# Decay attention and a spectral mix on one core: the fold's x sum moved to VectorE, 64-row blocks paired, the last unit half by rows, repeats in fp32

## The chip, the cores and the metric

One core of a Trainium2 chip runs the whole program, in one launch. Its engines are TensorE (PE in the profile; its weight loads are PEld), VectorE (DVE), ScalarE (ACT), GpSimd (POOL) and SyncE (SP), each with its own instruction queue, in order. GpSimd and SyncE issue the DMA transfers, which 16 DMA engines carry out. The metric is the device time of the program in microseconds; lower is better. A trace of one profiled execution goes with it.

## The reference

Attention with a decaying bias over 8 batches, 8 heads, 576 positions and head size 64, then a spectral mix over the 512 channels:

```python
scores = q @ k.T / sqrt(64) + (cum[i] - cum[j])      # cum: running sum of log f; causal
x = softmax(scores) @ v                               # (8, 576, 512) over all heads
X = rfft(x, axis=1)[:, :64]                           # 64 modes, Xr and Xi
Yr = Xr @ w_r[m] - Xi @ w_i[m];  Yi = Xr @ w_i[m] + Xi @ w_r[m]     # one 512x512 pair a mode
y = irfft(Y, n=576)
u = x + y
out = u + max(u @ w_ch, 0)
```

w_r and w_i have 64 x 512 x 512 fp32 numbers each, 134 MB together; q, k and v have 28 MB, the output 9.4 MB.

## The kernel before

**Tiles and blocks.** The 576 positions are four blocks of 128 and one of 64 (`SBLK`, block index sb or sc, 0 to 4). Heads go in pairs; `pairs` lists 32 of them, g over the four head pairs (128 channels each), b over the batches inside. x lies in `x_all[128, g, b, block, 128]` in bf16. Weights come in units of four modes (u, 0 to 15) and quarters of the 512 input channels (dc, 0 to 3). All loads are cast from fp32 to bf16 on the way.

**Order.** The schedule is written by hand: each engine runs its instructions in the order in which the Python text makes them.

**Attention stage** (L597 to L667, 34 iterations). Iteration i first issues loads on GpSimd (`load_qk(i + 4)`, one or two halves of a weight quarter by `issue_half`, `load_v(i + 3)`). Then come, interleaved: `trans` (q and k turned by PE, copied to `qkT` by VectorE, L391), `scores` (PE L466, exponential by ScalarE L473), `turn_v` (v turned into `tv` by PE, L413, and copied to `vT` by VectorE, L415; `vT` has one buffer), `back_v` (PE turns `vT` back block by block, L424 and L431, the 64-row block in two pieces; ScalarE copies to `vs`, L435), `av` (scores times values for the pair before), `norm` (VectorE divides by the row sums into `x_all`, L529), `dft` (PE, L545 and L566: the modes of x) and, from iteration 10, `spec_early`: weight quarters that are already there are multiplied into partial sums kept in `yacc`. The 64-row block of each batch lies in rows 0 to 63.

**Loads.** `wseq` is the order of the weight quarters. `issue_w` issues one quarter as one transfer of 1024 KB (in bf16), or in halves in the attention stage; the very last one in four parts, one a mode. `cuts` splits three quarters at a row. At most eight transfers of GpSimd's are under way: each issue waits for the landing of the one eight before.

**Spectral stage** (L844 to L932). For each unit the remaining quarters are multiplied as they land (`spec_mms`, PE L230: eight matmuls that write rows of A; the last unit uses `spec_cols`, PE L242: 32 matmuls that write columns). VectorE adds the early partial sum (Yb, L901), PE turns the result (L906), VectorE copies it to `YT` or `YLa` (L915, L918). Meanwhile `xw(b)` computes XW = x @ w_ch for each batch. From unit 12 on, ahead of each quarter but the last, `folds` works off a list: for each batch `fold_modes` (y_sb and yw_sb: the first 96 spectral columns and their product with w_ch, PE L754 and L765, ScalarE copies L762 and L773), then for each block `fold_u` (PE adds x by an identity matmul, L781, and the 96 columns, L784; ScalarE copies the sum back to `x_all`, L791) and, one block later, `fold_z` (PE L800; VectorE adds to XW, L807). Their PSUM results use four banks (`psX`). `SHARE`, `PART` and `MODES` say how much of the list each call takes. `place` puts the 64-row blocks of two batches into the lower and upper half of one block, here for the results only.

**The last quarter** comes in four parts. Between the parts PE does the identity matmuls of the first output steps (`base_mm`, L701), each several times over ("repeats": the result of the last counts). When the last part has been multiplied, VectorE adds it to the sums (L889, `accT`), and PE turns the last 32 spectral columns (`last_modes`).

**Output stage** (L1003 to L1045, 18 steps of two blocks). U = x + y and Z = u @ w_ch are completed on PE (`base`: x or XW by an identity matmul; `rest`: the last columns, L966), ScalarE copies U (L1000), VectorE makes max(Z, 0) + U (L1030), SyncE issues the store (L1045). In the steps of `late_x` one block's x is not added by PE but by GpSimd (L1035); in those of `by_pool` GpSimd makes one block's final sum (L1025).

Of the kernel before, what the change touches and what calls it, by code (L numbers as in the profile page):

```python
# [23 lines left out]
def kernel(  # L24
# [11 lines left out]
    nc = tc.nc  # L36
# [46 lines left out]
    wT = const.tile([128, NPAIR, 9], BF16, name="wT")  # L83
# [62 lines left out]
    cuts = {(4, 2): 30, (7, 2): 20, (10, 2): 20}  # L146
# [5 lines left out]
    def issue_w(half=None):  # L152
# [29 lines left out]
        elif half != 1:  # L182
            src = (moe_w_r, moe_w_i)[dc - 2]
            parts = [(0, 4, 0, 128)]
            if n + 1 == len(wseq):
                parts = [(j, 1, 0, 128) for j in range(4)]
            elif (u, dc) in cuts:
                n0 = cuts[(u, dc)]
                parts = [(0, 4, 0, n0), (0, 4, n0, 128)]
# [86 lines left out]
    nc.vector.tensor_scalar(s_f[:], s_f[:], float(S - 1), None, ALU.min)  # L276
# [30 lines left out]
    def setup_w():  # L307
# [7 lines left out]
        for hp in range(2):  # L315
            half = slice(64 * hp, 64 * hp + 64)
            nc.scalar.activation(wT[:, :, hp:8:2], cbg[:, :, 0:4, hp], ACT.Exp, scale=-1.0)
            nc.scalar.activation(wT[half, :, 8], cbg[half, :, 4, hp], ACT.Exp, scale=-1.0)
# [88 lines left out]
    def turn_v(i):  # L407

        tv = psM.tile([128, 9, 64], BF16, tag="m", name="tv")
        for r in range(9):  # L410
# [3 lines left out]
        st[i]["vT"] = vTpool.tile([128, S], BF16, tag="vT", name="vT")  # L414
        nc.vector.tensor_copy(  # L415
            st[i]["vT"][:].rearrange("p (c r) -> p c r", r=9), tv[:].rearrange("p r c -> p c r")
        )

    def back_v(i):

        vT = st[i]["vT"]
        vp = psM.tile([128, 9, Dh], BF16, tag="m", name="vp")
        for jb in range(4):
            nc.tensor.transpose(  # L424
                vp[:, 2 * jb : 2 * jb + 2, :].rearrange("p h d -> p (h d)"),
                vT[:, jb * 128 : jb * 128 + 128],
                ident_bf[:, :],
            )
        for hp in range(2):
            sl = slice(64 * hp, 64 * hp + 64)  # L430
            nc.tensor.transpose(vp[sl, 8, :], vT[sl, 512:576], ident_bf[sl, sl])  # L431
        vs = vspool.tile([128, 9, Dh + 1], BF16, tag="vs", name="vs")
        st[i]["vs"] = vs
        nc.vector.tensor_copy(vs[:, :, Dh : Dh + 1], _strided(wT[:, widx(i), :], [[1, 9], [1, 1]]))
# [8 lines left out]
    def scores(i, T):  # L443

        QT, KT = st[i]["T"][:, 0, :], st[i]["T"][:, 1, :]
        if T == 0:
            st[i]["et"] = epool.tile([128, 3, 2, 512], BF16, tag="et", name="et")
            st[i]["e4"] = epool.tile([128, 64], BF16, tag="e4", name="e4")
# [53 lines left out]

    def av(i, sb):
# [6 lines left out]
        Ms = SBLK[sb]  # L510
        for hp in range(2):
            for jb in range(sb + 1):
                rhs = vs[:, 8, :] if jb == 4 else vs[:, 2 * jb + hp, :]
                nc.tensor.matmul(  # L514
                    pav[:Ms, sb % 3, hp, :],
                    lhsT=eblk(i, hp, jb, sb),
                    rhs=rhs,
# [4 lines left out]
    def norm(i, part):  # L522
        g, b = pairs[i]
        pav = st[i]["pav"]
        for ns, lo, hi in ([(128, 0, 3)] if part == 0 else [(128, 3, 4), (64, 4, 5)]):
            n = hi - lo
            rcp = normsb.tile([128, 3, 2, 1], F32, tag="rcp", name="rcp")
            nc.vector.reciprocal(rcp[:ns, 0:n, :, :], pav[:ns, lo % 3 : lo % 3 + n, :, Dh : Dh + 1])
            nc.vector.tensor_tensor(  # L529
                x_all[:ns, g, b, lo:hi, :].rearrange("p s (h d) -> p s h d", h=2),  # L530
                pav[:ns, lo % 3 : lo % 3 + n, :, 0:Dh],
                _strided(rcp[:ns, 0:n, :, :], [[2, n], [1, 2], [0, Dh]]),
# [3 lines left out]
    def dft(i):  # L536
        g, b = pairs[i]
        if g < 2:
            pd = psM.tile([128, 3, 3, ML], F32, tag="m", name="pd")
            half = slice(64 * g, 64 * g + 64)  # L540
            for r in range(3):
                for sc in range(NSB):
                    ns = SBLK[sc]
                    xs = x_all[:ns, g, b, sc, :]
# [3 lines left out]
                        rhs=bas3[:ns, sc, :, ML:NM] if r else bas3[:ns, sc, :, 0:ML],  # L548
# [14 lines left out]
        for r in range(2):  # L563
            for sc in range(NSB):
                ns = SBLK[sc]
                nc.tensor.matmul(  # L566
                    pd[half, r, :, :],
                    lhsT=x_all[:ns, g, b, sc, r:128:2],
                    rhs=bas3[:ns, sc, :, :],
# [9 lines left out]
    def spec_early(u, dc):  # L579
        if u == NU - 1:  # L580
            AT = psM.tile([128, NEB, 8, B], F32, tag="m", name="AT0")
            spec_cols(AT, dc)
            nc.vector.tensor_copy(accT[:], AT[:].rearrange("p e c b -> p e b c"))
            return
# [491 lines left out]
```

## Time and profile before

| What | us |
|---|---|
| runs: all three | 435.54, 437.68, 676.76 |
| median | 437.68 |
| profiled execution | 435.24 |
| its span, first to last instruction | 433.5 |
| attention stage (copies of `vs`, L435, first and last start) | 21.0 to 226.6 |
| fold stretch (first and last L807) | 347.8 to 395.2 |
| first output transfer issued | 404.5 |
| last compute instruction ends | about 427.3 |

```profile
PE 359.8 (83%) x4444; PEld 198.8 (46%) x4444; DVE 265.4 (61%) x651; ACT 228.7 (53%) x374; POOL 143.1 (33%) x214
DMA 46%; PE 33%; DVE 11%; ACT 5%; issue 3%; POOL 1%; DVEq 0%; ACTq 0%; POOLq 0%
HBM read 163.73 MB, written 9.44 MB: 399 GB/s over the span
```

The first line has the busy time of each engine, its share of the span and its instructions; a busy PE is not a PE at its peak, since matmuls overlap. The second is the chain of work that ended last, followed back from the end: what it waited for, as shares of the span. In the answers by window the columns are: start and end, length, then busy us (and instructions) of PE, PEld, DVE, ACT and POOL, the granted TensorE clock (1.00 is full speed), the mean busy share of the 16 DMA engines, and GB/s. In the groups of instructions they are: line, engine, operation, output and inputs, shape and count, then busy us and mean ns of one, then the engine's idle time just before, and who ended it. In the order of time: start, duration, engine, line, operation, count.

### The profile page before, as it was taken

The numbers are of one execution on the slowest core, as the hardware profiler recorded it, in microseconds if no ns is written. First come the engines' busy times: TensorE is split into PE (matmuls) and PEld (weight loads), VectorE is DVE, ScalarE is ACT, GpSimd is POOL, SyncE is SP. The second block draws the span as 40 slices with busy tenths as digits, with TensorE's granted clock in tenths as the row PEclk, the third lists the DMA queues.
The fourth block names the chain that finished last, engine by engine and source line by source line (L and its number), as shares of the span: only waits on it lengthen the run. The fifth ranks groups of instructions, "written<-read, shape, count | busy, mean of one in ns | idle before, by whom it ended". The sixth has DMA issues, their size and how long they took to land.

```text
span 433.5 us, 10703 instructions
## 1 busy us (share of the span) xinstructions
PE 359.8 (83%) x4444; PEld 198.8 (46%) x4444; DVE 265.4 (61%) x651; ACT 228.7 (53%) x374; POOL 143.1 (33%) x214
## 2 busy tenths in 40 slices
PE   1689999988898899999987396599899599989992
PEld 0456666655665565665653132244343233434330
DVE  5788888776878797787785121222222256654893
ACT  4567667777775567667561022023133166752882
POOL 6444444444544444444304112112111212101272
PEclk9999999999999999999999589589799689999997
DMA  8999999999999999999999999999999999998597
GB/s 182 205 233 220 230 223 231 223 231 232 229 230 231 227 233 228 232 229 231 232 218 212 212 212 211 212 210 212 212 211 212 212 212 212 211 212 151 212 380 283
DMA packets 60785, 96.80 MB, mean 223 GB/s; under 512 B 4160, under 2 KB 29248, under 8 KB 60736
## 3 DMA queue, kind: packets, MB, share of 16 engines
q0 software_dynamic: 55040, 85.64, 103.9%
q1 hardware_dynamic: 5696, 10.47, 6.7%
q8 instruction: 35, 0.57, 0.5%
q14 instruction: 14, 0.11, 0.1%
HBM read 163.73 MB, written 9.44 MB: 399 GB/s over the span
## 4 chain that ended last, share of the span: by engine, by line
DMA 46%; PE 33%; DVE 11%; ACT 5%; issue 3%; POOL 1%; DVEq 0%; ACTq 0%; POOLq 0%
DMA w<-in_moe_w_i_dram 31%; DMA w<-in_moe_w_r_dram 13%; PE pd L545 5%; PE sps L466 5%; PE pav L514 5%; DVE qkT L391 4%; PE pd L566 3%; PE A L230 3%; ACT et L473 3%; PE tv L413 3%; DVE vT L415 2%; DMA qk<-in_k_dram 2%; DVE x_all L529 2%; PE Z L701 2%; PE U L701 2%
## 5 line engine op out<-in xcount | busy, mean ns | idle before, releaser
L473 ACT ACTIVATE et<-sps 128x1024 bf16<-128x1024 f32 x96 | 93.1, 1024 | 11.9 <-PE sps L466 10.1
L514 PE MATMUL pav<-vs,et 128*128 128x65 bf16 (+1 forms) x896 | 50.2, 195 | 15.6 <-ACT e L460 15.1
L514 PEld LDWEIGHTS <-et 128*128 128x128 bf16 (+1 forms) x896 | 38.8, 101 | 34.6 <-issue 32.6
L391 DVE COPY qkT<-tp 128x640 bf16<-128x640 bf16 x64 | 48.9, 765 | 4.0 <-PE tp L386 4.0
L901 DVE TENSOR_TENSOR Yb<-A,yx 128x512 bf16<-128x512 f32 x15 | 10.4, 692 | 60.0 <-PE A L230 59.9
L415 DVE COPY vT<-tv 128x576 bf16<-128x576 bf16 x32 | 24.2, 757 | 34.6 <-PE tv L413 33.9
L741 PE MATMUL pxw<-wch,xT 128*128 128x512 bf16 (+1 forms) x160 | 41.7, 417 | 0.0
L466 PE MATMUL sps<-qkT 64*128 64x512 bf16 (+4 forms) x320 | 38.8, 306 | 1.3 <-DVE qkT L391 1.1
L435 ACT COPY vs<-vp 128x576 bf16<-128x576 bf16 x32 | 20.4, 638 | 36.2 <-PE vp L431 36.2
L192 POOL DMA_DIRECT2D w<-in_moe_w_r_dram x19 | 13.9, 731 | 76.5 <-PE A L230 62.6
L529 DVE TENSOR_TENSOR x_all<-pav,rcp 128x384 bf16<-128x384 f32 (+2 forms) x96 | 36.2, 377 | 3.4
L230 PE MATMUL A<-w,XP 128*16 128x512 bf16 (+1 forms) x240 | 22.3, 453 | 19.0 <-DMA w<-in_moe_w_i_dram 11.8
L386 PE MATMUL tp<-ident_bf,qk 128*64 128x128 bf16 x576 | 29.3, 231 | 10.4 <-DMA qk<-in_k_dram 10.1
L748 ACT CAST XW<-pxw 128x512 bf16<-128x512 f32 (+1 forms) x16 | 9.3, 584 | 46.5 <-PE pxw L741 46.5
L748 ACT CAST yx<-pxw 128x512 bf16<-128x512 f32 (+1 forms) x24 | 14.0, 584 | 33.1 <-PE pxw L741 33.1
L112 POOL DMA_DIRECT2D qk<-in_q_dram x32 | 19.5, 608 | 34.1 <-PE tp L386 8.1
L791 ACT CAST x_all<-pu 128x512 bf16<-128x512 f32 (+1 forms) x40 | 23.4, 584 | 13.6 <-PE pu L784 12.9
L192 POOL DMA_DIRECT2D w<-in_moe_w_i_dram x19 | 13.4, 704 | 43.0 <-PE A L230 36.6
L741 PEld LDWEIGHTS <-xT 128*128 128x128 bf16 (+1 forms) x160 | 15.7, 108 | 22.6 <-issue 9.0
L112 POOL DMA_DIRECT2D qk<-in_k_dram x32 | 19.4, 605 | 18.1 <-DMA w<-in_moe_w_i_dram 5.9
L386 PEld LDWEIGHTS <-qk 128*64 128x64 bf16 x576 | 19.0, 113 | 13.6 <-issue 9.6
L403 DVE TENSOR_TENSOR vn<-vt,wn 128x576 bf16<-128x576 f32 x32 | 23.8, 744 | 1.9 <-ACT wn L328 1.9
(158 smaller groups left out, 693.9 us busy)
## 6 DMA issues: line engine op xcount, KB each, us to landing
w<-in_moe_w_i_dram POOLq DMA_DIRECT2D x19, 1024.0 KB, 31.6
w<-in_moe_w_r_dram POOLq DMA_DIRECT2D x13, 1024.0 KB, 29.5
w<-in_moe_w_r_dram POOLq DMA_DIRECT2D x23, 512.0 KB, 11.2
w<-in_moe_w_i_dram POOLq DMA_DIRECT2D x19, 512.0 KB, 11.0
out_dram<-o_sb SPq DMA_DIRECT2D x36, 256.0 KB, 2.8
vt<-in_v_dram POOLq DMA_DIRECT2D x29, 288.0 KB, 10.7
qk<-in_q_dram POOLq DMA_DIRECT2D x32, 144.0 KB, 10.7
qk<-in_k_dram POOLq DMA_DIRECT2D x32, 144.0 KB, 10.6
```

The source lines that it names most:

```text
L112: nc.gpsimd.dma_start(qk[64 * n : 64 * n + 64, :, :], src[b, 2 * g : 2 * g + 2, :, :].rearrange("h (p r) d -> p h (r d)", p=64),)
L192: nc.gpsimd.dma_start(w8[p0:p1, j : j + step, :, :].rearrange("p m r e -> p m (r e)"), src[m : m + step, 256 + 2 * p0 : 256 + 2 * p1, :].r ...
L230: nc.tensor.matmul(A[32 * j : 32 * j + M, :], lhsT=lhsT, rhs=rhs, start=st_, stop=sp_)
L386: nc.tensor.transpose(tp[64 * hp : 64 * hp + 64, r - r0, :, :].rearrange("p n c -> p (n c)"), qk[:, hp, r * 64 : r * 64 + 64], ident_bf[:, :],
L391: nc.vector.tensor_copy(st[i]["T"][:].rearrange("p n (c r) -> p n c r", r=9)[:, :, :, r0:r1], tp[:, 0 : r1 - r0, :, :].rearrange("p r n c ...
L403: nc.vector.tensor_tensor(vn[:], st[i]["vt"][:], _strided(wn[:, widx(i), :], [[1, 9], [0, Dh]]), ALU.mult)
L415: nc.vector.tensor_copy(st[i]["vT"][:].rearrange("p (c r) -> p c r", r=9), tv[:].rearrange("p r c -> p c r"))
L466: nc.tensor.matmul(ps[:, hp, c : c + n], lhsT=KT[sl, jb * 128 : jb * 128 + 128], rhs=QT[sl, i0 : i0 + n], start=True, stop=True,)
L473: nc.scalar.activation(st[i]["et"][:, T, :, :], ps[:], ACT.Exp, scale=scale)
L514: nc.tensor.matmul(pav[:Ms, sb % 3, hp, :], lhsT=eblk(i, hp, jb, sb), rhs=rhs, start=(jb == 0), stop=(jb == sb),)
L529: nc.vector.tensor_tensor(x_all[:ns, g, b, lo:hi, :].rearrange("p s (h d) -> p s h d", h=2), pav[:ns, lo % 3 : lo % 3 + n, :, 0:Dh], _stri ...
L741: nc.tensor.matmul(pxw[rows, :], lhsT=xT[:, eb, sb * 128 : sb * 128 + Ms], rhs=wch[:, eb, :], start=(eb == 0), stop=(eb == NEB - 1),)
```

## The change

Seven edits:

- `fold_u`: the identity matmul and ScalarE's copy go; VectorE adds the PSUM result to `x_all` in place. The 64-row blocks of two batches are folded as one block of 128 rows (`modes_to` makes two matmuls for it), in `fold_u` and in `fold_z`.
- For this `place` holds from the attention on: odd batches have their 64-row block in rows 64 to 127 of the even batch's block. `vT` gets 64 more columns, a copy of its last 64 made by GpSimd, so that `back_v` is five full transposes; `wT` and `vs` have ten parts instead of nine; the basis is set up for both halves. `xw` takes a 64-row pair with the odd batch (640 columns or 512 in place of 576).
- The last unit: quarters 0 and 1 by rows (`spec_mms`) into an fp32 sum Yf, turned by four fp32 matmuls (`ypf`) into `accT`; quarters 2 and 3 by columns as before.
- Repeats: `again`, an fp32 matmul of 256 columns, in place of repeated bf16 ones.
- `late_x` has three more steps: 4, 7 and 16.
- `cuts`: two quarters in three parts in place of three quarters in two.
- `SHARE` 19.1 in place of 19.8, with the pairs put into the list behind their odd batch.

```diff
-    cuts = {(4, 2): 30, (7, 2): 20, (10, 2): 20}
+    cuts = {(5, 3): (54, 126), (8, 3): (63, 78)}
...
-        st[i]["vT"] = vTpool.tile([128, S], BF16, tag="vT", name="vT")
+        st[i]["vT"] = vTpool.tile([128, S + 64], BF16, tag="vT", name="vT")
...
+        nc.gpsimd.tensor_copy(st[i]["vT"][:, S : S + 64], st[i]["vT"][:, S - 64 : S])
...
-        for jb in range(4):
+        for jb in range(NSB):
             nc.tensor.transpose(
...
-        for hp in range(2):
-            sl = slice(64 * hp, 64 * hp + 64)
-            nc.tensor.transpose(vp[sl, 8, :], vT[sl, 512:576], ident_bf[sl, sl])
...
-        Ms = SBLK[sb]
+        rows, _ = place(pairs[i][1], sb)
...
-                    pav[:Ms, sb % 3, hp, :],
+                    pav[rows, sb % 3, hp, :],
...
+            def modes_to(ps, b, sb, which):
+
+                for c in (b, b + 1) if sb == NSB - 1 else (b,):
+                    rows, _ = place(c, sb)
+                    nc.tensor.matmul(
+                        ps[rows, :],
+                        lhsT=BI[:KF, sb * 128 : sb * 128 + SBLK[sb]],
+                        rhs=ys[c][which][:KF, :],
+                        start=True,
+                        stop=True,
+                    )
+
             def fold_u(b, sb):
 
-                Ms = SBLK[sb]
-                rows, to = place(b, sb)
                 pu = psX.tile([128, D], F32, tag="x", name="pu")
-                nc.tensor.matmul(
-                    pu[rows, :], lhsT=ident_bf[:Ms, :Ms], rhs=x_all[:Ms, :, b, sb, :], start=True, stop=False
-                )
...
-                nc.scalar.copy(
-                    x_all[rows, :, to, sb, :], pu[rows, :].rearrange("p (g c) -> p g c", g=NEB)
-                )
+                modes_to(pu, b, sb, 0)
+                xb = x_all[:, :, b, sb, :]
+                nc.vector.tensor_tensor(xb, pu[:].rearrange("p (g c) -> p g c", g=NEB), xb, ALU.add)
 
             def fold_z(b, sb):
...
+                modes_to(pz, b, sb, 1)
+                nc.vector.tensor_tensor(XW[b][:, sb, :], pz[:], XW[b][:, sb, :], ALU.add)
...
-            SHARE = 19.8
-            work = [(b, sb) for b in range(B) for sb in range(-1, NSB)]
+            SHARE = 19.1
+            work = [(b, sb) for b in range(B) for sb in range(-1, NSB - 1)]
+            for p in range(B // 2):
+                work.insert(11 * p + 10, (2 * p, NSB - 1))
...
+            def again(ps):
+
+                nc.tensor.matmul(
+                    ps[:, 0:256], lhsT=ident_f[:], rhs=Yf[:, 0:256], start=True, stop=True
+                )
...
+                        ypf = bank(psT, "ypf")[:, 0 : 64 * NEB].rearrange("p (e c) -> p e c", e=NEB)
+                        for eb in range(NEB):
+                            nc.tensor.matmul(
+                                ypf[:, eb, :],
+                                lhsT=Yf[:, eb * 128 : (eb + 1) * 128],
+                                rhs=perm_f[:],
...
+                        nc.vector.tensor_copy(accT[:], ypf.rearrange("p e (b c) -> p e b c", b=B))
                         U0 = [bank(psT, "U0") for _ in range(2)]
-                        for n in range(4):
-                            base_mm(U0[n % 2], 0, n % 2, 0, True)
-                    if last:
+                    if last and dc == 1:
+                        A = psA.tile([128, D], F32, tag="a", name="A1")
+                        spec_mms(A, u, dc, True, True)
+                        Yf = xtp.tile([128, D], F32, tag="yf", name="Yf")
+                        nc.vector.tensor_tensor(Yf[:], A[:], yacc[u // 2][:, u % 2, :], ALU.add)
+                    elif last:
...
                                 if j == 1:
-                                    for stop in (True, False):
-                                        for k in range(2):
-                                            base_mm(U0[k], 0, k, 0, stop)
+                                    again(U0[0])
+                                    for k in range(2):
+                                        base_mm(U0[k], 0, k, 0)
...
-        late_x = (3, 5, 6, 9, 10, 11, 12, 13, 14)
+        late_x = (3, 4, 5, 6, 7, 9, 10, 11, 12, 13, 14, 16)
```

## The prediction

> **What bounds the kernel now.** I read the page's slices first, then two-microsecond windows around the end, the order of time there, the groups of instructions between 342.5 and 400 us, and the list of DMA issues. The profiled execution took 435.24 us (span 433.5, and 1.7 around it); the three runs shown have a median of 437.68, with 435.54 the lowest. Sums are made on 435.24.
>
> ```profile
> DMA  8999999999999999999999999999999999998597
> GB/s 182 205 233 220 230 223 231 223 231 232 229 230 231 227 233 228 232 229 231 232 218 212 212 212 211 212 210 212 212 211 212 212 212 212 211 212 151 212 380 283
> ```
>
> The DMA engines are full from the second slice to about 398 us: the stream of weights, q, k and v is the bound, and no edit to an engine's work shortens it. What follows is a second DMA-bound stage, the output (share, then GB/s, are the last two columns):
>
> ```profile
> 396.00:398.00 2.00, 2.00 (x41) 1.22 (x38) 0.42 (x1) 0.00 (x0) 0.00 (x0) 1.00 0.93 173
> 398.00:400.00 2.00, 1.97 (x21) 0.71 (x16) 0.00 (x0) 0.00 (x0) 0.00 (x0) 1.00 0.20 38
> 402.00:404.00 2.00, 2.00 (x11) 0.59 (x10) 0.91 (x2) 1.29 (x4) 0.00 (x0) 1.00 0.04 8
> 406.00:408.00 2.00, 2.00 (x15) 0.62 (x11) 1.51 (x3) 1.94 (x5) 1.15 (x1) 1.00 1.03 378
> 428.00:430.00 2.00, 0.00 (x0) 0.00 (x0) 0.00 (x0) 0.00 (x0) 0.00 (x0) 0.50 1.02 380
> ```
>
> The 36 output transfers (9.44 MB at 380 GB/s, 24.8 us) run nearly without a hole from 405.7 us. So the time is: end of the loads, plus the idle valley between, plus the output. Only the valley can be moved, and it begins when the last weight quarter is multiplied and VectorE takes it up:
>
> ```profile
> 400.23 0.41 PE L242 MATMUL AT<-XP,w 128*128 128x16 bf16 x8
> 400.68 0.29 DVE L889 TENSOR_TENSOR YLa<-AT,accT 128x128 bf16<-128x128 f32 x1 [3.67 <-PE AT L242]
> ```
>
> The step at 400.68 waits for the last landing alone. Whatever makes it later moves the end one for one.
>
> **Change, part by part: the folds.** Between 342.5 and 400 us the first 96 spectral columns are folded into x and XW:
>
> ```profile
> L791 ACT CAST x_all<-pu 128x512 bf16<-128x512 f32 (+1 forms) x40 | 23.4, 584 | 13.6 <-PE pu L784 12.9
> L807 DVE TENSOR_TENSOR yx<-pz,yx 128x512 bf16<-128x512 f32 (+1 forms) x24 | 16.4, 691 | 6.8 <-PE pz L800 6.5
> L807 DVE TENSOR_TENSOR XW<-pz,XW 128x512 bf16<-128x512 f32 (+1 forms) x16 | 11.0, 691 | 11.7 <-PE pz L800 11.6
> 346.20:399.90 53.70, 52.04 (x362) 21.66 (x360) 31.52 (x51) 31.04 (x55) 6.30 (x12) 0.97 1.08 204
> ```
>
> Removed: 40 identity matmuls (about 0.22 us apart, 8.6 us of PE) and 40 ScalarE copies (23.4 us). Added: x is added by VectorE, at the shape of L807 (PSUM fp32 plus bf16). Pairing 64-row blocks makes 36 of 40 on each side: 72 VectorE adds for 40. The 40 took 27.4 us, 0.685 each; 72 take 49.3, 21.9 more. VectorE was busy 31.5 of these 53.7 us; now 53.4. PE, full here (52.0 of 53.7), falls to about 43; but PE was waiting for weights already (0.9 us before 385.1, 0.7 before 390.3), so that saving buys nothing, while VectorE has become full.
>
> When does VectorE finish? ScalarE's first fold copy is at 346.54 now; the identity matmul before it, 0.4 at that clock, goes, so VectorE's first add comes at 346.1. From there: 49.3 of adds, three Yb adds (0.69 each, 2.1), three pairs of L918 copies (0.48, 1.4), the new fp32 Yf add (0.7): 53.5, gapless to 399.6. Gaps: VectorE waits wherever PE starts a batch's modes or first meets a load that VectorE's lag held up; I allow 1.5, between 0 and 3. VectorE ends the folds at 401.1, where it ended at 395.9.
>
> PE is in order and has four PSUM banks for fold results, so it can be at most about three adds ahead: its last fold ends at 399.0 (394.4 before). Behind it are queued: four fp32 matmuls into ypf, the 32 columns of the third block (1.2 us), and the last block in four parts with repeats between. The only fp32 matmuls in the trace (L323, 64 columns) take 0.32 alone, four within 0.73; ypf costs 0.75. Repeats: 9 instead of 17 matmuls, four of them fp32 with 256 columns. By L323's spacing (0.18 for 64 columns) one is 0.73; by four bf16 passes of 256 columns, at L701's 0.22 us for 512, it is 0.43. I take 0.43, since L323's short matmuls carry a fixed part; 0.73 adds 0.9. Before, repeats filled the 1.2 us between two landings and cost nothing; now all quarters have landed when PE comes and everything lies in series: 399.0 + 0.75 + 1.2 + four parts at 0.3 + three repeats at 0.43 + four base matmuls at 0.22 = 404.3. The step of 400.68 (L887 in the changed kernel) starts at 404.5: **3.8 us later** (2.3 to 6.2 with the gaps and the fp32 price).
>
> **Last unit by rows.** The fifteenth unit's first two blocks take 8 row matmuls (0.65 us) instead of 32 column matmuls (1.1); both stand in other work's shade, no term.
>
> **Tail.** Three more steps let GpSimd add x (1.16 us a step, before nine such and three L1025): three PE matmuls fewer, 0.65 us. GpSimd gets 3.5 us in a stage of 24, and its last add comes near 427, while transfers queue until 431. The output stage is full of DMA; the one dip (share 0.88 in 422 to 424) is worth 0.24. Term: -0.2 (0 to -0.5).
>
> **Attention.** Back_v loses one transpose of six, scores and sums stay: 0.2 us per iteration, off the bound. Added: a GpSimd copy of vT's last 64 columns, priced between 0.1 and L925's 0.34 (three times the columns); I take 0.2, 6 us in all on an engine that issues the loads. The copy stands in POOL's queue behind the iteration's load issues and before the next ones; PE's back_v waits for it. In the iteration at 40 us the last load is issued at 46.87 to 47.6, while back_v ran at 44.63: PE will stand some 3 us there, and stay 3 to 6 us later than now. What covers it:
>
> ```profile
> w<-in_moe_w_i_dram POOLq DMA_DIRECT2D x19, 1024.0 KB, 31.6
> qk<-in_k_dram POOLq DMA_DIRECT2D x32, 144.0 KB, 10.6
> ```
>
> Loads are issued 10.6 us before they land in this stage, 31 us in the next: the engines have that much queued. A POOL that waits 3 to 5 us for VectorE's vT leaves the queue filled. Term 0; with the cover gone, a few of these waits would reach the stream, up to 8 us.
>
> **Load parts.** Other weights are cut, into three parts. The 0.93 and 0.20 in the windows above show that the 16 engines end apart: at an even finish the stream would end near 398.1 instead of 400. A row more or less on one engine is 0.62 us (1024 KB at 212 GB/s, 4.95 us for 8 rows each). I bound the last landing by -1.9 and +2.5; up to 3 us later it is hidden under VectorE, and earlier it buys nothing. The Trainium skill, "DMA: Bandwidth & Descriptors", section "Why a DMA increments its semaphore by 16 and not by 1", says a transfer uses the largest number of engines up to 16 that divides its rows, from a moving cursor, so parts of 54, 72 and 2 rows would use 9, 12 and 2; that speaks against such cuts, no view here names the engines, and the sum would be the same.
>
> **Sum:** 435.24 + 3.8 - 0.2 = **438.8 us**.
>
> **Rivals.** *The adds fit* (not slower). If VectorE's adds cost less beside an idle ScalarE, or the stretch starts sooner, the last landing decides again. The point: VectorE must end 3.8 us sooner, 3.8 / 72 = 0.053 less per add, 0.63 or below. For it: L1030 (two fp32 inputs, 512 columns) runs 0.62 apart at the end. Against: 40 adds of this very form lie between 681 and 696 ns. Time: 435.24 - 0.2, and up to 1.9 less by an even finish: 434.2. Chance 0.20.
>
> *The clock drops* (slower). PE now waits for banks:
>
> ```profile
> 304.70:308.10 3.40, 1.64 (x22) 0.68 (x20) 1.12 (x2) 0.58 (x1) 0.76 (x1) 1.00 1.12 212
> 383.20:386.60 3.40, 2.48 (x17) 0.88 (x15) 2.48 (x4) 1.41 (x4) 0.00 (x0) 1.00 1.12 213
> ```
>
> After the first window (PE busy 0.48) the granted clock was 0.5 until 315; after the second (0.73) it stayed 1. In the new stretch PE is at 43 of 53.7, 0.8, with windows of folds alone near 0.55 (a 0.38 us matmul per 0.69 us add). At half clock L784 takes 0.63 for 0.38, so a load's PE work, 43 / 11 = 3.9, becomes 6.5, over the 4.95 between loads: half the stretch so is +8.5, and a slow entry into the tail +2: 449. Chance 0.09. The Trainium skill, "TensorE: Matmul & The Clock Gate", "HAM oscillation", warns of PE-idle gaps over 3.4 us; by that rule this stretch, whose gaps are under 1 us, keeps its clock, but the first window above had no such gap and lost it. I keep the chance of the row.
>
> *GpSimd's copies reach the stream*: 438.8 + 6 = 445, from waits over 10 us on. Chance 0.04. That the change does other than it says can be left out: the new program's order has the 72 adds.
>
> **Numbers.** Forecast 438.8, chance 0.67, own range 437 to 441.5. The range takes in the rival below, short of its full even finish, and the copies above: 433.5 to 445. A measurement of this kernel tells about 2%, 8.7 us, from no change: forecast and first rival lie within; the clock rival (0.09) and a part of the copies lie above. Faster 0.02, same 0.86, slower 0.12.
>
> **What would show it.** Right: VectorE over 95% busy from 346 to 400, its last fold add at 400 or later, L887 starting near 404.7, PE waiting on pu and pz banks. Wrong: adds below 0.63, L887 within 1 us of the last landing, a granted clock under 1 between 350 and 425, a DMA share under 1 before 395, output transfers with holes.

## The result and the profile after

| | before | changed |
|---|---|---|
| median of 9 runs each, us | 435.02 | 438.91 |
| ratio to before, 95% interval | | 1.0082 (1.0056 to 1.0108) |
| profiled execution / its span | 435.24 / 433.5 | 439.19 / 437.3 |
| last landing of a weight | 400.18 | 400.88 |
| TensorE's last fold ends | 394.67 | 397.02 |
| VectorE's last fold add ends | 395.86 | 398.72 |
| VectorE takes up the last quarter (L889; L887) | 400.68 | 405.49 |
| first output transfer issued; last one landed | 404.50; 432.53 | 409.48; 436.38 |

The changed kernel is 0.8% slower, 3.9 us, a difference that the runs tell from no change and that lies within 2%. One run of each, at 676.76 and 456.44 us, lies far above the others, and the ratio leaves it out. The page's slices of the changed kernel (40 slices of its span):

```profile
PEclk9999699999999999999999588599699698985997
DMA  8999999999999999999999999999999999995498
GB/s 186 205 234 220 232 220 232 231 226 230 232 231 227 233 226 234 226 233 227 237 212 211 212 212 212 202 212 210 198 212 212 212 212 212 211 213 100 164 381 322
```

The load stream is full to the same place as before, slice 36; then comes a hole that is wider (100 and 164 GB/s, where one slice of 151 stood alone), and the output at 381 GB/s. The loss is in the valley. The row of the clock has a dip there (the 5; the 8 ahead of it is a shorter one at 381.6 to 385.0) that was not in the kernel before. The windows of the changed kernel show it (start and end, length, busy us and instructions of PE, PEld, DVE, ACT and POOL, granted clock, DMA share, GB/s); from the second line on they are the stretches of 3.41 us at whose bounds the granted clock changes:

```profile
346.20:399.90 53.70, 45.07 (x278) 18.49 (x276) 47.99 (x84) 8.73 (x15) 6.31 (x12) 0.88 1.10 207
391.86:395.27 3.41, 1.97 (x15) 0.61 (x14) 3.41 (x8) 0.00 (x0) 1.22 (x4) 1.00 1.11 208
395.27:398.68 3.41, 3.40 (x13) 2.07 (x13) 3.41 (x6) 0.00 (x0) 0.00 (x0) 0.50 0.96 178
398.68:402.09 3.41, 3.41 (x55) 2.49 (x55) 0.89 (x3) 0.00 (x0) 0.00 (x0) 0.50 0.20 36
402.09:405.51 3.42, 3.20 (x23) 2.14 (x24) 0.02 (x1) 0.00 (x0) 0.00 (x0) 0.50 0.00 0
405.51:408.92 3.41, 3.41 (x20) 1.43 (x21) 1.85 (x8) 1.78 (x4) 0.00 (x0) 1.00 0.02 5
```

VectorE is the full engine of the fold stretch, as forecast (48.0 of 53.7 us; 31.5 before), and PE has 45.1 for 52.0. But in 391.86 to 395.27 PE is busy for 1.97 of 3.41 us, and for the next 10.2 us its clock is 0.5. That is just the work that nothing hides: the end of the folds and the last unit. The order of time on VectorE, then on PE (start, duration, engine, line, operation, count, and in brackets idle time before and what ended it):

```profile
394.45 0.68 DVE L781 TENSOR_TENSOR x_all<-pu,x_all 128x512 bf16<-128x512 f32 x1
395.05 0.68 DVE L787 TENSOR_TENSOR yx<-pz,yx 128x512 bf16<-128x512 f32 x1
395.64 0.68 DVE L781 TENSOR_TENSOR x_all<-pu,x_all 128x512 bf16<-128x512 f32 x1
405.49 0.29 DVE L887 TENSOR_TENSOR YLa<-AT,accT 128x128 bf16<-128x128 f32 x1 [5.25 <-PE AT L240]
...
395.18 0.60 PE L768 MATMUL pu<-y_sb,BI 96*64 96x512 bf16 x2 [1.21 <-DVE x_all L781]
395.78 1.24 PE L768 MATMUL pz<-yw_sb,BI 96*128 96x512 bf16 x3
396.95 1.97 PE L844 MATMUL ypf<-perm_f,Yf 128*128 128x64 f32 x8
398.71 1.28 PE L240 MATMUL AT<-XP,w 128*128 128x16 bf16 x40
399.82 1.20 PE L826 MATMUL U<-Yf,ident_f 128*128 128x256 f32 x2
405.03 0.42 PE L240 MATMUL AT<-XP,w 128*128 128x16 bf16 x8
```

Two things to see. The adds last 0.68 us each, yet start 0.60 us apart: one begins before the one before it has ended. And PE, once let go by VectorE at 395.18, ends its folds at 397.02, runs ypf for 1.97 us and each pair of fp32 instructions for 1.20; the last quarter had landed at 400.88, long before PE's last L240. The groups of the fold stretch (busy us, mean ns of one, idle time before) give the adds' duration again, the same as before's L807:

```profile
L781 DVE TENSOR_TENSOR x_all<-pu,x_all 128x512 bf16<-128x512 f32 x36 | 24.5, 683 | 5.6 <-PE pu L768 5.3
L787 DVE TENSOR_TENSOR yx<-pz,yx 128x512 bf16<-128x512 f32 x22 | 14.9, 681 | 0.0
```

Off the bound, the attention went as foreseen. PE's wait for vT's extra columns shows in the order of time:

```profile
48.19 0.29 PE L421 MATMUL vp<-ident_bf,vT 128*128 128x128 bf16 x1 [3.09 <-POOL vT L414]
```

The attention ends about 4 us later (last copy of `vs` at 230.5, 226.6 before), and the list of DMA issues still has the loads queued 10 and 29 us ahead:

```profile
w<-in_moe_w_i_dram POOLq DMA_DIRECT2D x17, 1024.0 KB, 29.5
...
qk<-in_k_dram POOLq DMA_DIRECT2D x32, 144.0 KB, 10.3
```

### The profile page after: what moved, and what is told of

It reads as the page before. It is cut to its first block, busy times and chain, and to the rows that moved or that the text cites. A ratio compares the mean times of both kernels' runs of the same rounds, so it can differ in the third digit from the quotient of the medians.

```text
span 437.3 us, 10340 instructions
## 1 busy us (share of the span) xinstructions
PE 343.5 (79%) x4282; PEld 195.3 (45%) x4293; DVE 284.8 (65%) x684; ACT 205.7 (47%) x329; POOL 154.8 (35%) x250
## 4 chain that ended last, share of the span: by engine, by line
DMA 35%; PE 34%; DVE 16%; issue 7%; POOL 3%; ACT 3%; POOLq 0%; DVEq 0%; ACTq 0%
DMA w<-in_moe_w_r_dram 15%; DMA w<-in_moe_w_i_dram 13%; DMA x_all<-in_moe_w_i_dram 5%; PE pd L545 4%; DVE qkT L387 4%; PE sps L460 4%; PE A L228 4%; PE pav L513 4%; DMA wch<-in_moe_w_ch_dram 3%; DVE x_all L781 3%; PE pd L566 2%; DVE vT L411 2%; PE tv L409 2%; PE pyw L753 2%; DVE yx L787 2%
## 5 line engine op out<-in xcount | busy, mean ns | idle before, releaser
L429 ACT COPY vs<-vp 128x640 bf16<-128x640 bf16 x32 | 22.3, 697 | 35.5 <-PE vp L421 35.5
L729 PE MATMUL pxw<-wch,xT 128*128 128x512 bf16 x136 | 34.8, 401 | 1.1 <-DVE xT L721 0.7
L190 POOL DMA_DIRECT2D w<-in_moe_w_i_dram x23 | 15.8, 689 | 51.3 <-DMA w<-in_moe_w_i_dram 22.3
L190 POOL DMA_DIRECT2D w<-in_moe_w_r_dram x16 | 12.0, 748 | 54.2 <-DMA w<-in_moe_w_r_dram 19.8
L736 ACT CAST yx<-pxw 128x512 bf16<-128x512 f32 x22 | 12.9, 586 | 34.1 <-PE pxw L729 34.1
L781 DVE TENSOR_TENSOR x_all<-pu,x_all 128x512 bf16<-128x512 f32 x36 | 24.5, 683 | 5.6 <-PE pu L768 5.3
L721 DVE COPY xT<-ptr 128x512 bf16<-128x512 bf16 (+1 forms) x32 | 13.8, 455 | 21.9 <-PE ptr L718 21.2
L736 ACT CAST XW<-pxw 128x512 bf16<-128x512 f32 x14 | 8.2, 586 | 41.8 <-PE pxw L729 26.6
```

Of the source, the lines that this page charges most:

```text
L190: nc.gpsimd.dma_start(w8[p0:p1, j : j + step, :, :].rearrange("p m r e -> p m (r e)"), src[m : m + step, 256 + 2 * p0 : 256 + 2 * p1, :].r ...
L729: nc.tensor.matmul(pxw[:], lhsT=xT[:, eb, sb * 128 : sb * 128 + 128], rhs=wch[:, eb, :], start=(eb == 0), stop=(eb == NEB - 1),)
L781: nc.vector.tensor_tensor(xb, pu[:].rearrange("p (g c) -> p g c", g=NEB), xb, ALU.add)
```

## The experiments

The theories. **A**: the clock; VectorE's adds leave TensorE idle, the granted clock goes to 0.5 as the folds end, and the work left takes twice its time. **B**: VectorE's lag, the forecast's own; the folds end late, and the rest stands in series behind them. **C**: the fp32 instructions (turn and repeats) are what is long (the expectation of run 2 calls something else C: that the repeats hold the clock up). **D** and **E** came later: D, that PE's series behind the folds counts at any clock, E, that the remaining edits (cuts, rows, GpSimd) cost something. Each ratio is to the kernel before, run on the same chip (medians 435.02, 434.84, 435.33 and 435.25 for the four groups of runs), with its 95% interval.

**1. Busy folds.** Ahead of each of the 36 x folds an idle matmul into the same bank, whose result is overwritten.

```diff
                 pu = psX.tile([128, D], F32, tag="x", name="pu")
+                nc.tensor.matmul(
+                    pu[:], lhsT=ident_bf[:], rhs=x_all[:, :, b, sb, :], start=True, stop=True
+                )
                 modes_to(pu, b, sb, 0)
```

> The changed kernel, with a bf16 identity matmul of 512 columns put ahead of each fold_u whose result is overwritten: PE gets back the 36 matmuls (0.22 us each, 7.8 us) that the change took from the fold stretch, VectorE and ScalarE do what they do in the changed kernel. Theory A (clock): the drop to half speed at 395.3 lengthened PE's chain between the folds and the first output. Then the granted clock is 1.00 from 395 to 405, ypf takes 0.75 us instead of 1.97, a repeat 0.43 instead of about 1.0, L887 (here six lines lower) starts near 402.3 instead of 405.5, and the time is some 3 us under the changed kernel's 438.9: 435.5 to 436.5. Theory B (the forecast: VectorE's adds hold PE back): VectorE's adds are as before, 0.60 apart, so the step stays at 405 and the time at 438 to 439.5.

Measured: 437.26, ratio 1.0052 (1.0033 to 1.0072). The windows of its trace:

```profile
393.33:396.75 3.42, 2.26 (x14) 1.30 (x14) 3.42 (x7) 0.00 (x0) 0.84 (x3) 1.00 1.11 207
396.75:400.16 3.41, 3.41 (x55) 2.49 (x54) 1.87 (x4) 0.00 (x0) 0.00 (x0) 0.50 0.59 112
```

PE was still idle for a third of the window in which it waits for the last banks (no idle matmul stands ahead of the XW folds), so the clock went again, later and for 6.8 us instead of 10.2. L887's step came at 403.62. The median moved towards A, by 1.7 us, but its interval overlaps the changed kernel's: not decisive.

**2. No repeats.** The four calls of `again` removed (the result of none is used).

```diff
-                                    again(U0[0])
                                     for k in range(2):
                                         base_mm(U0[k], 0, k, 0)
...
```

> The changed kernel without its four fp32 repeats. Theory A (clock): at half speed each costs about 1.0 us and three stand ahead of the last quarter's last part, so the step of VectorE after it starts near 402.5 instead of 405.5, still at clock 0.5; but the first output steps then meet the half clock too, which gives back 0 to 2 us: 436 to 438. Theory B (forecast): three at 0.43, 1.3 us less: 437.6. Theory C (the repeats keep the clock up): without them the clock stays at 0.5 well into the output stage, and the time is 439 or more.

Measured: 438.00, ratio 1.0056 (1.0035 to 1.0077), not told apart from the changed kernel. In its trace the clock is 0.5 from 397.31 to 404.14 and the step comes at 404.30. From the end of the last fold (398.95, 1.9 us later than in the changed kernel) to the step are 5.35 us, where the changed kernel, its clock at 0.5 as well, has 8.47. So at half clock the three repeats ahead of the last part are some 3.1 us of what is long, and C is a part of it; the medians, 0.9 us apart, do not settle how large. That the repeats hold the clock up did not show: without them it was back at 1 from 404.14.

**3. x back on TensorE and ScalarE**, blocks still paired.

```diff
-                modes_to(pu, b, sb, 0)
-                nc.vector.tensor_tensor(xb, pu[:].rearrange("p (g c) -> p g c", g=NEB), xb, ALU.add)
+                nc.tensor.matmul(pu[:], lhsT=ident_bf[:], rhs=xb, start=True, stop=False)
+                modes_to(pu, b, sb, 0, False)
+                nc.scalar.copy(xb, pu[:].rearrange("p (g c) -> p g c", g=NEB))
```

> The changed kernel with fold_u's sum put back on PE (identity matmul) and ScalarE (copy); blocks stay paired, all else as changed. Theories A and B agree: VectorE is at some 27 us of 54 in the fold stretch, PE full, clock 1.00, the folds end near 394, and the step after the last quarter starts at the last landing, 401.3: 434.5 to 436. If the fp32 turn and the repeats alone were the cause (theory C), it would stay at 437.5 or more.

Measured: 437.18, ratio 1.0036 (1.0018 to 1.0055). The profiled execution was the fastest of its twelve, 434.74: folds done on PE at 393.55, clock 1 from 347 to 429, and the step at 400.67, where the kernel before has it. That execution gives back all of the valley, as A and B both have it, with ypf and the fp32 repeats still in the kernel, so that C alone is not the cause. The median, 2.2 us above before, does not give it back, and the slower executions left no trace. Nine of the twelve (435.87 and more) have a mean clock of 0.919 to 0.933, the three faster ones 0.932 to 0.939, too coarse to say where it fell.

**4. The old cuts** in the changed kernel.

```diff
-    cuts = {(5, 3): (54, 126), (8, 3): (63, 78)}
+    cuts = {(4, 2): (30,), (7, 2): (20,), (10, 2): (20,)}
```

> The changed kernel with the load parts of before, (4, 2), (7, 2) and (10, 2) cut at rows 30, 20 and 20. Theories A and B agree: the last landing comes at about 400.2 instead of 400.9 and GB/s shows no dip to 202 and 198 in the slices around 275 and 310, but PE comes to the last quarter after that anyway, so the time stays within 0.5 us of the changed kernel's 438.9. Rival: the stream's end decides after all, then 0.7 to 1.2 us less.

Measured: 438.76, ratio 1.0077 (1.0047 to 1.0106): no difference. Its traced execution, 441.87, is the slowest of the six. Its last landing is at 401.25, where 400.2 was expected, and the first of the 16 engines to end its share of that transfer does so at 394.9; in the changed kernel these are 400.9 and 397.1. Over all traces the first and the last end lie 5.7 to 7.5 us apart with the old cuts (four traces) and 2.9 to 4.4 with the new ones (ten): the new cuts do even the finish out, but in the changed kernel VectorE's step is 4.6 us behind it.

**5. Busy to the end.** Idle matmuls ahead of all 72 folds, and the kernel before's bf16 repeats in place of the fp32 ones.

```diff
                 pz = psX.tile([128, D], F32, tag="x", name="pz")
+                nc.tensor.matmul(
+                    pz[:], lhsT=ident_bf[:], rhs=x_all[:, :, b, sb, :], start=True, stop=True
+                )
                 modes_to(pz, b, sb, 1)
...
```

> The changed kernel with an idle bf16 identity matmul ahead of each of the 72 folds (x and XW), and with the kernel before's 17 bf16 repeats in place of the fp32 ones, so that TensorE is busy through the folds and between the last landings; all of VectorE's 72 adds stay. Theory A (the adds cost nothing by themselves; a granted clock of 0.5 in the valley, brought on by an idle TensorE, costs the time): no granted clock under 1 between 385 and 420 us, the step L887 at 401 to 402, 435.0 to 436.0 us. Theory B (VectorE's lag, the forecast's): the folds end where they did, L887 at 404 or later, 438 to 439.5. Theory D (TensorE's work in the tail, ypf and the rest, is in series whatever the clock): clock 1, L887 at 403 to 404, 437 to 438.

Measured: 440.34, ratio 1.0112 (1.0084 to 1.0139): slower still by the median, with intervals that overlap, and a miss for A as it stood. Two windows and three moments of its trace:

```profile
346.30:400.90 54.60, 52.04 (x306) 21.18 (x305) 48.24 (x82) 8.14 (x14) 6.32 (x12) 0.98 1.06 200
396.40:399.80 3.40, 2.22 (x10) 0.70 (x9) 3.40 (x6) 0.00 (x0) 0.36 (x2) 1.00 0.51 94
```

```profile
399.63 0.41 PE L768 MATMUL pz<-yw_sb,BI 96*64 96x512 bf16 x2
399.97 1.10 PE L850 MATMUL ypf<-perm_f,Yf 128*128 128x64 f32 x8
...
406.30 0.29 DVE L896 TENSOR_TENSOR YLa<-AT,accT 128x128 bf16<-128x128 f32 x1 [2.92 <-PE AT L240]
```

The clock is 1 from 348.55 us on, and ypf takes 1.10 us. But PE has 52 us of work again beside 48 of VectorE's; each now waits for the other, the folds end 3 us later, at 400.04, and 6.3 us of work at full clock stand behind them. This is B and D, made pure: with the folds' end at 400 the forecast's series costs more than the changed kernel loses.

**6. Run 3 with the kernel before's bf16 repeats.**

```diff
-                                    again(Z0[0])
-                                    for k in range(2):
-                                        base_mm(Z0[k], 0, k, 1)
+                                    for stop in (True, False):
+                                        for k in range(2):
+                                            base_mm(Z0[k], 0, k, 1, stop)
...
```

> The third experiment (x added by TensorE and ScalarE, blocks paired) with the kernel before's 17 bf16 repeats in place of the fp32 ones. That experiment's profiled execution had the clock at 1 through the valley and took 434.74, while its median was 437.18. Theory A (the other executions lost the clock, because four fp32 repeats leave TensorE idle between landings): 434.4 to 435.2 with a spread under 2 us, the clock at 1 in the valley. Theory E (what is left of the change, load parts, rows, GpSimd's sums, costs 2 us): 436.5 to 437.5, as before.

Measured: 435.64, ratio 1.0021 (0.9998 to 1.0044), 434.0 to 438.4. The median is 1.5 us below that of run 3, towards A, but the intervals overlap, and the spread did not go. Theory E's 436.5 to 437.5 is not borne out: cuts, rows, GpSimd's sums and pairing together cost too little to be told from nothing (the interval leaves room for up to 1.9 us).

**7. The kernel before without its repeats.** 12 of the 17 matmuls between the last landings are gone (the expectation says 10); the five whose result counts stay.

```diff
-                        for n in range(4):
-                            base_mm(U0[n % 2], 0, n % 2, 0, True)
...
-                                    for stop in (True, False):
-                                        for k in range(2):
-                                            base_mm(Z0[k], 0, k, 1, stop)
+                                    for k in range(2):
+                                        base_mm(Z0[k], 0, k, 1)
...
```

> The kernel before with its repeated matmuls of the last unit gone (10 of 17 base matmuls, the ones whose result is written again). Theory A: TensorE is nearly idle from 395 to 400 us, the clock goes to 0.5 in many executions, and 2 to 4 us are lost: 436.5 to 439. Theory B: TensorE waits for the last landing there anyway, 435.0 within 0.5.

Measured: 436.94, ratio 1.0043 (1.0025 to 1.0061). Less work, and 2.1 us slower. Windows and the first output issue (SPq is SyncE's DMA queue) of its trace:

```profile
396.60:400.02 3.42, 2.37 (x42) 1.25 (x38) 0.42 (x1) 0.00 (x0) 0.00 (x0) 1.00 0.75 140
400.02:403.43 3.41, 2.38 (x20) 1.19 (x17) 1.01 (x6) 0.58 (x1) 0.00 (x0) 0.50 0.04 8
403.43:406.84 3.41, 3.41 (x11) 0.70 (x10) 1.24 (x2) 2.15 (x4) 0.00 (x0) 0.50 0.00 0
```

```profile
407.01 2.05 SPq L1038 DMA_DIRECT2D out_dram<-o_sb  x3
```

PE's repeats fill the waits between the last landings; without them the clock falls at 400.02, and the valley's second half, from VectorE's step at 401.38 to the first output issue, takes 5.6 us instead of 3.8. Nothing of VectorE's load is in this kernel: an idle PE alone does it, here too at a busy share of 0.69.

**8. The kernel before with more GpSimd sums.**

```diff
-        late_x = (3, 5, 6, 9, 10, 11, 12, 13, 14)
+        late_x = (3, 4, 5, 6, 7, 9, 10, 11, 12, 13, 14, 16)
```

> The kernel before with the change's list of steps whose x is added by GpSimd (12 for 9), nothing else. The forecast's term for the tail: 0.2 us less (0 to 0.5), 434.5 to 435.0. By the changed kernel's output stage, which ran 1.0 us shorter than before's: 434.0 to 434.2. If GpSimd's steps come late: over 435.4.

Measured: 434.82, ratio 0.9999 (0.9980 to 1.0019). In its trace the output takes 27.4 us from first issue to last landing, 28.0 in the kernel before and 26.9 in the changed one. The term is too small to be seen in the time.

**9. vT's copy on VectorE** in the changed kernel.

```diff
-        nc.gpsimd.tensor_copy(st[i]["vT"][:, S : S + 64], st[i]["vT"][:, S - 64 : S])
+        nc.vector.tensor_copy(st[i]["vT"][:, S : S + 64], st[i]["vT"][:, S - 64 : S])
```

> The changed kernel with the copy of vT's last 64 columns on VectorE in place of GpSimd, nothing else. The forecast's price for that copy was 0, covered by the loads in the queue: 438.9 us within 0.6, vs(4) back at 45 to 46 us from 48.5, the last landing within 0.7 us of 400.9. If GpSimd's wait does reach the stream: a last landing 1 us or more earlier and 437.5 to 438.

Measured: 438.96, ratio 1.0076 (1.0049 to 1.0104), last landing 401.25: no difference from the changed kernel that can be told, so the copy's place costs little if anything. The expected move of `vs` in the fifth iteration did not show (48.2): no wait of PE over 0.5 us is left there, but this execution lost the clock at 35 us and was 3 us late by the iteration before.

**10. Idle work in the last folds.** Run 5 had put idle matmuls where they hold up folds. Here they stand in the last call alone, in a bank of their own.

```diff
+                scr = bank(psT, "scr") if all_ else None
+
+                def idle():
+
+                    if all_:
+                        nc.tensor.matmul(
+                            scr[:], lhsT=ident_bf[:], rhs=x_all[:, :, 0, 0, :], start=True, stop=True
+                        )
...
+                    idle()
                     fold_u(b, sb)
...
+                        idle()
                         fold_z(*late.pop(0))
...
```

> The changed kernel, where only the last call of the folds (about ten of them, from 392 us on, where TensorE waits for banks) gets one idle bf16 identity matmul each, into a PSUM bank of its own, so that it fills TensorE's waits and takes no bank from VectorE. The folds should end where they do in the changed kernel (TensorE's last at 396.5 to 397.5). Theory A (the clock in the valley costs most of the 3.9 us): the granted clock stays 1 from 388 to 420, the row from the last fold to L887 takes 5.0 us in place of 8.5, L887 at 401.3 to 402.3, 435.3 to 436.3 us. Theory B (the folds' end and the work in series behind it cost it, the clock changes little): L887 at 404 or later, 438 to 440. The busy folds of the run before last kept the clock and were no faster, but moved the folds' end to 400; here it should stay.

Measured: 436.77, ratio 1.0023 (1.0000 to 1.0046): 2.1 us under the changed kernel's median, and the intervals do not meet. Windows, then the order of time on PE and VectorE:

```profile
393.05:396.46 3.41, 2.75 (x19) 1.05 (x17) 3.41 (x8) 0.00 (x0) 1.22 (x4) 1.00 1.09 202
396.46:399.87 3.41, 3.41 (x51) 2.43 (x50) 3.41 (x7) 0.00 (x0) 0.00 (x0) 1.00 0.49 91
```

```profile
397.49 0.41 PE L768 MATMUL pz<-yw_sb,BI 96*64 96x512 bf16 x2
397.83 1.10 PE L856 MATMUL ypf<-perm_f,Yf 128*128 128x64 f32 x8
398.77 1.40 PE L240 MATMUL AT<-XP,w 128*128 128x16 bf16 x40
...
403.35 0.29 DVE L899 TENSOR_TENSOR YLa<-AT,accT 128x128 bf16<-128x128 f32 x1 [2.66 <-PE AT L240]
```

PE is busy for 2.75 us of the window, the clock holds, and from the end of the last fold (397.90) to VectorE's step are 5.45 us, where the changed kernel has 8.47. VectorE's adds are all there, so the clock is shown as the larger part. The step is still 2.9 us behind the last landing (400.43), later than A had it; this rest is B's and D's. The traced execution, 437.83, is the third slowest of the twelve; the faster ones left no trace.

**11. Run 10 with the last unit by columns and bf16 repeats**, so without ypf.

```diff
-                    if last and dc == 1:
-                        A = psA.tile([128, D], F32, tag="a", name="A1")
-                        spec_mms(A, u, dc, True, True)
...
-                    elif last:
+                    if last:
...
```

> The run above with the last unit again by columns and the kernel before's 17 bf16 repeats, so no fp32 matmul (ypf, 1.0 us at full clock) stands between the last fold and the last parts; of the folds' change all is kept. Theory A: nothing but the clock counts, L887 within 0.5 us of the run above. Theory D (what stands in series behind the last fold counts): 1.0 us for ypf less and about 1 us for the longer repeats more, so the same time, 435 to 436.5, and L887 5 us behind the last fold. With the clock at 0.5 all the same: 438 to 440.

Measured: 435.77, ratio 1.0014 (0.9996 to 1.0031), not told apart from run 10; last fold on PE at 397.01, step at 402.35, 5.3 us later, clock 1 from 385 to 430. D's arithmetic: ypf's microsecond is given back by the longer repeats.

**12. Run 11 with the last pair of batches' x on TensorE and ScalarE.** The identity matmul stands where the idle one stood.

```diff
+                if b >= 6:
+                    nc.tensor.matmul(pu[:], lhsT=ident_bf[:], rhs=xb, start=True, stop=False)
+                    modes_to(pu, b, sb, 0, False)
+                    nc.scalar.copy(xb, pu[:].rearrange("p (g c) -> p g c", g=NEB))
+                    return
```

> The run before with x of the last pair of batches (9 of the 36 steps) added as in the kernel before, by an identity matmul and a ScalarE copy; the matmul stands where the idle one stood, so TensorE's work stays and VectorE loses 9 adds (5.4 us by the 0.60 spacing). Theory B for what is left (VectorE's folds still end late): TensorE's last fold at 394 to 395.5, L887's step within 0.7 us of the last landing, 434.3 to 435.2 us. Theory D (what TensorE has in series): the last fold 1 us earlier at most, the step over 1.2 us behind the last landing, 435.5 to 436.5. With a granted clock of 0.5 in the valley: 437 and more.

Measured: 435.52, ratio 1.0010 (0.9988 to 1.0033). Its order of time:

```profile
394.11 0.41 PE L773 MATMUL pz<-yw_sb,BI 96*64 96x512 bf16 x2
...
401.24 0.41 PE L240 MATMUL AT<-XP,w 128*128 128x16 bf16 x8 [1.45 <-DMA w<-in_moe_w_i_dram]
401.49 0.59 PE L703 MATMUL U<-x_all,ident_bf 128*128 128x512 bf16 x2
...
401.69 0.29 DVE L896 TENSOR_TENSOR YLa<-AT,accT 128x128 bf16<-128x128 f32 x1 [4.74 <-PE AT L240]
```

Nine adds fewer on VectorE, and the folds end at 394.52, PE waits for a landing again, and the step follows the last landing (401.19) by 0.5 us, as in the kernel before. So what was left in the trace of run 11 was VectorE's lag. The times of runs 11 and 12 are not told apart (their intervals overlap), nor is either from the kernel before. No version was faster than it.

## Why the prediction was right, and where not

**The time was right, 438.8 for 438.91, and so was the place; the mechanism was only in part.** The forecast put 3.8 us into the step at 400.68; it moved by 4.8. What bounds the kernel, the output's length and the three terms taken as about nothing (attention, cuts, tail) held: runs 4, 8 and 9 show no difference that can be measured. The tail came out 1.1 us shorter in the trace where 0.2 was forecast, which took back the 1.0 us that the step was over, but run 8 doesn't show the time of it. Over all traces the output takes 28.0 and 28.1 us with the old list of steps (the kernel before and run 7) and 26.9 to 27.8 with the new one (twelve).

**The price of an add, 0.685, failed.** It was taken from the duration of one (681 to 696 ns), and 72 of these were laid end to end. They start 0.60 us apart. In the trace of before PE paced the adds, so that none stood back to back for long; the one row that spoke, L1030 at 0.62 apart (at its closest 0.598), was quoted for the rival and outweighed. From its first add to its last VectorE worked for 47.5 us, not 53.5.

Two other terms took back part of these 6 us. The first add came at 347.04, not 346.1, and VectorE waited for PE for 4.2 us, where 1.5 was allowed and 3 at most. The longest wait stands behind a stretch of half clock (381.6 to 385.0):

```profile
385.67 0.69 DVE L781 TENSOR_TENSOR x_all<-pu,x_all 128x512 bf16<-128x512 f32 x1 [1.54 <-PE pu L768]
```

So VectorE ended the folds at 398.72, not 401.1, and PE its last at 397.0, not 399.0. Where the same folds were traced again they ended later: VectorE at 400.65, 401.31 and 399.57 in runs 2, 4 and 9, after 6.4, 6.4 and 4.6 us of waits. Executions that reach the forecast's end so reach it by the waits, not by the price. The rival's own point, 0.63 or below, was met, and its time, 434.2, did not come: with the later start and the waits VectorE's end moved by 2.4 us, where the rival needed 3.8, and it took for granted that the rest of the valley would run at full clock.

The Trainium skill has the duration of an add right: "VectorE: DVE Perf Modes", section "The TRN2 errata — SBUF-src ops pay a fixed extra latency per instruction", gives (N + 151) / 0.96 for an fp32 add of N elements, which is 691 ns for 512; the adds of the traces, with one fp32 and one bf16 input, take 681 to 691 ns on average. The distance between two in a row is smaller by 0.08 us, and for a row of them that is what counts.

**The clock, taken at a chance of 0.09, was the larger part.** The rival had the mechanism (PE waits for banks, a window of low activity, then 0.5), and its price for "a slow entry into the tail", 2 us, was near: run 10 gives 2.1 by the medians and 3.0 by the two traces (5.45 for 8.47). Its 8.5 us for half of the stretch at half clock did not come; beside the valley and the stretch's first 1.3 us (in the kernel before 2.9) the clock was low for only 6.8 us, in two pieces (361.1 to 364.6 and 381.6 to 385.0). Had the clock held in the profiled execution, the step would have come at about 397.0 + 5.45 = 402.5 (an estimate from that trace and run 10's), 1.8 us later than before, and the forecast of 3.8 would have been too high. The folds' end, forecast 2 us too late, and the missing 3.0 us of clock cancelled, all but 1.0 us. That the time agreed is luck.

**What is in series behind the last fold was sized right**: 5.5 forecast (399.0 to 404.5), 5.45 in run 10 at full clock. ypf was 0.94 instead of 0.75, a pair of fp32 instructions 0.51 apart at full clock against 0.43.

The forecast weighed a rule of the Trainium skill, "TensorE: Matmul & The Clock Gate", section "HAM oscillation": no idle gap over 3.4 us, no loss of clock. The trace goes against it: the longest wait of PE in the window that lost the clock was 1.21 us. The same part of the page tells of a second case ("A second HAM failure mode: psum-queue depth-cycling"), matmuls of 512 columns that cycle through PSUM banks with many short waits, and says that the clock oscillates there too; that case describes these folds, and the prediction passed it over.

**What would show it**, as the prediction listed it: VectorE over 95% busy was 89%; the last add at 400 or later was 398.7; L887 near 404.7 was 405.5; PE waiting for banks was so; and two of its signs of error, adds below 0.63 and a clock under 1 between 350 and 425, stood in the trace while the time agreed.

**Open**: the changed versions with the valley closed in the trace (runs 3, 6, 12) still have executions up to 438, more of them than the kernel before. These left no trace; that they too lose the clock somewhere is a guess, not shown.

## What to carry to other kernels

Price a row of like instructions by the distance between their starts where they stand back to back, not by the duration of one, and look in the trace for a stretch where nothing else paces them. When a change takes work off TensorE beside a full engine or a full stream, work out its busy share over each few microseconds up to the next stretch that nothing hides; idle matmuls there can be worth more than the time they take (run 7). In run 10 they wrote a bank that nobody waits for and gained; in run 5 they wrote the folds' own banks and did not, but that run differs in their number and in the repeats too, so the bank is not shown to be the reason. And a time that comes out as forecast is no proof of the reasons: here errors of 2 and 3 us nearly cancelled, and only the trace told.

## What the runs showed of the hardware

- The granted clock is decided in stretches of 3.41 us, and not by long gaps: over the 14 traces of this case (60 to 424 us, stretches at full clock), every stretch with PE busy for less than 0.48 of it was followed by a clock of 0.5, none with 0.77 or more, and between these it went both ways (0.66 lost it in run 1, 0.63 kept it in run 5).
- VectorE's adds of 128x512 (PSUM fp32 and SBUF bf16, to bf16) start 0.598 us apart back to back while each lasts 0.68.
- At the granted 0.5 some matmuls of the valley took about twice as long and others no longer (changed kernel against run 10): eight fp32 instructions of 64 columns 1.97 us for 1.10, two bf16 matmuls of 512 columns (L698) 1.06 for 0.59, but 40 bf16 matmuls of 16 columns (L240) 1.28 for 1.40.
